# A linear-attention block with a ReLU feed-forward layer: the first four tiles loaded and normalized in another order, tile 4 transposed on TensorE, all engines' orders written anew

## The chip, the cores and the metric

The kernel runs on one core of a Trainium2 chip. The metric is device time in microseconds; a time given for a kernel is the median of its runs.

## What is computed

The input is 2048 rows of 512 bf16 values. With layer norm without weights:

```python
x = A_x
h = x + attention(layernorm(x), A_wqkv, A_wo)
h2 = h + relu(layernorm(h) @ B_w1) @ B_w2        # 512 -> 1792 -> 512

# attention, 32 heads of 16:
q, k, v = split(x @ wqkv)
phi = lambda t: where(t > 0, t + 1, exp(t)) + 1e-6
kv  = sum over rows of phi(k)^T v ;  z = sum over rows of phi(k)
o   = (phi(q) @ kv) / (phi(q) . z + 1e-6)
return o @ wo
```

## The kernel before

The 2048 rows are 16 tiles of 128 rows (128 partitions). Four tiles make a chunk of 512 rows, which is the moving operand of the matmuls that produce transposed results. Nothing is scheduled automatically: the text `ORDER` names every operation with its tile and its PSUM bank, and the program is recorded in that order. Each engine runs its own instructions strictly in that order and waits by semaphores for the others, so moving a word in the text moves it in one engine's queue (a DMA: in SyncE's) and past nothing else. A word such as `K.0.3.0.2` means operation `op_K` with tile 0, bank 3, and the contraction steps 0 and 1.

The first phase, up to about 40 us, goes through these operations for each tile t:

- `lx` (L201) loads x tiles, `lk`, `lq`, `lv`, `lo`, `l1`, `l2` (L204) load weights: wk, wq, wv, wo, w1, w2, each in halves or pieces. All DMAs are issued by SyncE (SP), in the order of the text.
- `S` (L226) and `A` (L227) on VectorE: statistics of a tile, and their aggregation to mean and variance. `R` (L232, L233) on ScalarE: the reciprocal of the standard deviation as exp(-0.5 ln(var + eps)), for one tile or for a pair in one instruction each. `N` (L251) on VectorE: the normalized tile.
- The tile transposed, as the matmuls need it: either `T` (L270), four transposes on TensorE into a PSUM bank, and `E` (L280), ScalarE's copy to SBUF; or `X` (L291), one DMA transpose issued by SyncE. Before the change tiles 0 to 3 go by T and E, tiles 4 to 15 by X.
- `K` (L299): four matmuls, k of the tile, into one of the banks 0 to 3. `F` and `U` on ScalarE (L317, L320): exp and relu of it, one bank or two at a time. `M` and `D` on VectorE (L324, L327): min(exp, 1) + 1e-6, and the sum with the relu, which is phi(k). `W` (L332) does U's and D's work in one VectorE instruction from PSUM.
- `G` (L351): four matmuls that add the tile's part of layernorm(x)^T phi(k) into the banks 4 to 7.

Ahead of the first tile `warm` (L215) does 11 matmuls on zeros. After the tiles, z and kv are formed (`z`, `kv`, `kx`), multiplied with wo (`m`), and q is computed per chunk (`Q`, L307, then `qF`, `qU`, `qM`, `qD` or `qW`, as for k). The reciprocal of the denominator is expanded to all columns by ScalarE (`dnx`, L461), transposed by DMA (`dt`, L480) or on TensorE (`rt`, copied by `re` or `rv`), and multiplied with phi(q) by VectorE (`dm`, L484); `h` (L494) multiplies that with the matrix of `m`, and `hD` (L500) adds x. The second layer norm is `s`, `a`, `r`, `n`, its transposes `x` (L292) or `t` and `e`. Then come `p` (L510, with w1), its relu `pA` on ScalarE or `pD` on VectorE (L521), `f` (L530, with w2), `fo` (L538) and the store `fd` (L545). Tile 15, the last, is done in three pieces of columns.

Of the kernel before, what the change touches and what calls it, by code (L numbers as in the profile page):

```python
# [56 lines left out]
def kernel(  # L57
# [18 lines left out]
    NT = S // P  # L76
# [11 lines left out]
    const = ctx.enter_context(tc.tile_pool(name="const", bufs=1))  # L88
    big = ctx.enter_context(tc.tile_pool(name="big", bufs=1))
# [11 lines left out]
    x_nat = big.tile([P, NT, D], BF16, name="x_nat")  # L101
# [6 lines left out]
    eps5 = const.tile([P, 1], F32, name="eps5")  # L108
# [8 lines left out]
    ln_nat = h_nat  # L117
# [10 lines left out]
    mv = big.tile([P, NT, nc.vector.BN_AGGR_DIM], F32, name="mv")  # L128
    rstd = big.tile([P, NT], F32, name="rstd")
    nmean = big.tile([P, NT], F32, name="nmean")  # L130
    st2 = big.tile([P, NT, nc.vector.BN_STATS_DIM], F32, name="st2")
    mv2 = big.tile([P, NT, nc.vector.BN_AGGR_DIM], F32, name="mv2")
    rstd2 = big.tile([P, NT], F32, name="rstd2")
# [5 lines left out]
    hn = big.tile([P, NQ, D], BF16, name="hn")  # L139
# [109 lines left out]
    def op_N(t, k=0, n=KD):  # L249
        cols = slice(k * P, (k + n) * P)  # L250
        nc.vector.tensor_scalar(  # L251
            out=ln_nat[:, t, cols], in0=x_nat[:, t, cols],
            scalar1=mv[:, t, 0:1], scalar2=rstd[:, t : t + 1],
            op0=ALU.subtract, op1=ALU.mult,
        )

    def op_n(t):
# [323 lines left out]
```

## Time and profile before

| what | us |
|---|---|
| median of 3 runs | 170.32 (169.92 to 170.33) |
| the profiled execution | 170.08 |
| its span, first to last instruction | 168.4 |
| TensorE busy | 162.7 (97%) |
| VectorE busy | 101.2 (60%) |
| ScalarE busy | 67.7 (40%) |

Times in the profile are microseconds from the start of the span. PE is TensorE, PEld its weight loads, DVE VectorE, ACT ScalarE, POOL GpSimd, SPq the queue on which SyncE issues DMAs. In the timelines a row has start, length, engine, line, operation, operands and count, and in brackets how long the engine had been idle before and what ended that. In the chain of waits a row has start, length and what held the end of the program at that time. In the list of DMA issues the last number is the time from issue to landing.

### The profile page before, as it was taken

To read this page: it belongs to the slowest core of one execution; us is meant where nothing else is said; L and a number is where in the kernel's file an instruction comes from. 1 tells how busy PE (TensorE), PEld (TensorE's weight loads), DVE (VectorE), ACT (ScalarE), POOL (GpSimd) and SP (SyncE) were. 2 spreads that over 40 slices of the span, in tenths; PEclk is the share of its full clock that TensorE was granted. 3 is DMA by queue.
4 is the path that set the end of the run, shared out by engine and by line. 5 is a ranking of instruction groups with operands and counts; after the bars stand their busy time and mean duration, and the time that the engine had idled before them with its cause. 6 is when DMAs were issued, how large, how long until landed. Compare 5 with 4: busy or idle time off the path is not lost.

```text
span 168.4 us, 2310 instructions
## 1 busy us (share of the span) xinstructions
PE 162.7 (97%) x871; PEld 76.1 (45%) x871; DVE 101.2 (60%) x202; ACT 67.7 (40%) x100; POOL 4.8 (3%) x21
## 2 busy tenths in 40 slices
PE   7699999999999999999999999999999999999993
PEld 2244443445554454544444444444444444444552
DVE  3899998997578999786967372047203600204152
ACT  3697765847879865652000504200220245000000
POOL 7300000000000000000000000000000000000000
PEclk9999999999999999999999999999999999999999
DMA  4954566899133353535130126300320000002113
GB/s 128 339 187 94 132 123 150 231 326 351 36 64 62 75 147 72 146 62 104 27 64 0 31 42 157 82 4 0 84 72 0 31 4 0 0 0 84 40 35 93
DMA packets 30491, 15.49 MB, mean 92 GB/s; under 512 B 23184, under 2 KB 29328, under 8 KB 30480
## 3 DMA queue, kind: packets, MB, share of 16 engines
q1 hardware_dynamic: 30480, 15.34, 34.5%
q8 instruction: 7, 0.11, 0.3%
q14 instruction: 4, 0.03, 0.1%
HBM read 7.86 MB, written 2.10 MB: 59 GB/s over the span
## 4 chain that ended last, share of the span: by engine, by line
PE 94%; DMA 2%; DVE 1%; SPq 0%; issue 0%
PE bk L530 29%; PE bk L510 29%; PE bk L299 9%; PE bk L351 8%; PE bk L307 8%; PE bk L494 8%; DMA x_nat<-in_A_x_dram 2%; PE bk L270 1%; PE bk L448 1%; DVE st L226 1%; PE bk L392 1%; PE bk L404 1%; SPq L201 0%; PE bk L370 0%; DVE gT L538 0%
## 5 line engine op out<-in xcount | busy, mean ns | idle before, releaser
L530 PE MATMUL bk<-w_sb,at 128*128 128x512 bf16 (+2 forms) x252 | 50.7, 355 | 0.0
L510 PE MATMUL bk<-lnT,w_sb 128*128 128x512 bf16 x224 | 50.5, 379 | 0.0
L516 ACT ACTIVATE at<-bk 128x1024 bf16<-128x1024 f32 x17 | 17.3, 1022 | 55.6 <-PE bk L510 55.6
L530 PEld LDWEIGHTS <-at 128*128 128x128 bf16 x252 | 23.5, 98 | 25.3 <-DVE at L521 0.2
L510 PEld LDWEIGHTS <-w_sb 128*128 128x128 bf16 x224 | 21.7, 98 | 26.0
L538 DVE SCALAR_TENSOR_TENSOR gT<-bk,rstd,h_nat 128x512 bf16<-128x512 f32 (+2 forms) x18 | 12.2, 690 | 31.2 <-PE bk L530 31.2
L521 DVE TENSOR_SCALAR at<-bk 128x1024 bf16<-128x1024 f32 x11 | 13.3, 1220 | 20.7 <-PE bk L510 20.4
L317 ACT ACTIVATE eb<-bk 128x1024 bf16<-128x1024 f32 (+1 forms) x18 | 16.6, 926 | 6.9 <-PE bk L299 4.2
L307 PE MATMUL bk<-lnT,wq_sb 128*128 128x512 bf16 x64 | 15.8, 379 | 0.0
L299 PE MATMUL bk<-wk_sb,lnT 128*128 128x512 bf16 x64 | 15.5, 380 | 0.0
L494 PE MATMUL bk<-m_sb,pqs 128*128 128x512 bf16 x64 | 15.3, 379 | 0.0
L351 PE MATMUL bk<-at,h_nat 128*128 128x512 bf16 x56 | 13.7, 379 | 0.0
L320 ACT ACTIVATE rb<-bk 128x1024 bf16<-128x1024 f32 (+1 forms) x14 | 12.5, 900 | 0.7 <-PE bk L307 0.7
L500 DVE TENSOR_TENSOR h_nat<-bk,x_nat 128x512 bf16<-128x512 f32 x16 | 10.6, 681 | 2.4 <-PE bk L494 2.3
L226 DVE BATCH_NORM_STATS2 st<-x_nat 128x6 f32<-128x512 bf16 x16 | 10.5, 681 | 2.4 <-DMA x_nat<-in_A_x_dram 2.4
L228 DVE BATCH_NORM_STATS2 st<-h_nat 128x6 f32<-128x512 bf16 x16 | 10.8, 684 | 0.1
L351 PEld LDWEIGHTS <-h_nat 128*128 128x128 bf16 x64 | 6.2, 97 | 7.7 <-issue 0.7
L299 PEld LDWEIGHTS <-lnT 128*128 128x128 bf16 x64 | 5.8, 98 | 8.2 <-DMA lnT<-h_nat 1.8
L494 PEld LDWEIGHTS <-pqs 128*128 128x128 bf16 x64 | 6.2, 98 | 7.0 <-DVE pqs L484 0.3
L307 PEld LDWEIGHTS <-wq_sb 128*128 128x128 bf16 x64 | 5.9, 98 | 6.4
L461 ACT ACTIVATE wk_sb<-ld 128x1024 bf16<-128x1024 f32 x8 | 8.1, 1051 | 0.1
L324 DVE TENSOR_SCALAR eb<-eb 128x1024 bf16<-128x1024 bf16 (+1 forms) x18 | 6.9, 383 | 0.9 <-ACT eb L317 0.8
(61 smaller groups left out, 89.0 us busy)
## 6 DMA issues: line engine op xcount, KB each, us to landing
out_dram<-gT SPq DMA_DIRECT2D x15, 128.0 KB, 1.9
w_sb<-in_B_w_dram SPq DMA_DIRECT2D x2, 896.0 KB, 8.4
x_nat<-in_A_x_dram SPq DMA_DIRECT2D x2, 512.0 KB, 6.6
w_sb<-in_B_w_dram SPq DMA_DIRECT2D x2, 512.0 KB, 4.6
x_nat<-in_A_x_dram SPq DMA_DIRECT2D x3, 256.0 KB, 4.2
w_sb<-in_B_w_dram SPq DMA_DIRECT2D x2, 384.0 KB, 3.4
wk_sb<-in_A_wqkv_dram SPq DMA_DIRECT2D x2, 256.0 KB, 4.0
wq_sb<-in_A_wqkv_dram SPq DMA_DIRECT2D x2, 256.0 KB, 3.0
```

What stands on the lines that cost most here:

```text
L226: op_S = lambda t: nc.vector.bn_stats(out=st[:, t, :], in_=x_nat[:, t, :])
L299: nc.tensor.matmul(bk[:, b, :], lhsT=lnT[c][:, kd, j * P : (j + 1) * P], rhs=wk_sb[:, kd, :], start=(kd == 0), stop=(kd == KD - 1),)
L307: nc.tensor.matmul(bk[:, b, :], lhsT=wq_sb[:, kd, j * P : (j + 1) * P], rhs=lnT[c][:, kd, :], start=(kd == 0), stop=(kd == KD - 1),)
L317: nc.scalar.activation(out=buf(eb, kind, i, n), in_=bank(at_bank[kind, i], n), func=ACT.Exp)
L320: nc.scalar.activation(out=buf(rb, kind, i, n), in_=bank(at_bank[kind, i], n), func=ACT.Relu)
L351: nc.tensor.matmul(bk[:, KD + kd, :], lhsT=ln_nat[:, t, kd * P : (kd + 1) * P], rhs=pk(t)[:, 0, :], start=(t == 0), stop=(t == NT - 1),)
L494: nc.tensor.matmul(bk[:, b, :], lhsT=pqs[:, (c * KD + jb) % NQ, j * P : (j + 1) * P], rhs=m_sb[:, jb, :], start=(jb == 0), stop=(jb == KD ...
L510: nc.tensor.matmul(bk[:, b, cols], lhsT=w1_sb[:, kd, f * P : (f + 1) * P], rhs=lnT[c][:, kd, cols], start=(kd == 0), stop=(kd == KD - 1),)
L516: nc.scalar.activation(out=acts[c % 2][:, f : f + n, :], in_=bank(at_bank["p", c, f], n), func=ACT.Relu)
L521: nc.vector.tensor_scalar(out=acts[c % 2][:, f : f + n, :], in0=bank(at_bank["p", c, f], n), scalar1=0.0, scalar2=None, op0=ALU.max,)
L530: nc.tensor.matmul(bk[:, b, 0 : w * P], lhsT=acts[c % 2][:, f, j * P : (j + 1) * P], rhs=w2_sb[:, f, k * P : (k + w) * P], start=(f == 0), ...
L538: nc.vector.scalar_tensor_tensor(out=o_t[:, t % NO, cols], in0=bk[:, at_bank["f", t, k], 0 : w * P], scalar=rstd2[:, t : t + 1], in1=h_nat ...
```

## The change

All tiles of the first phase go through the same operations as before, with these differences:

- Tiles 2 and 3 of x are loaded by one DMA each (`lx.2.1 lx.3.1`, before `lx.2.2`); the two halves of wk follow, now fifth and sixth in SyncE's queue.
- Tile 0 is aggregated, scaled and normalized ahead of the other tiles, and its transposes and the first half of its K stand ahead of the transposes of tile 1.
- R of tiles 2 and 3 is one pair (`R.2.2`, before `R.2.1 R.3.1`), and so are F, U, M and D of these two tiles (`F.2.2` and so on, before one bank at a time).
- Tile 4 is transposed by `T.4.3` and `E.4` instead of `X.4`.
- All queues stand in a new order to the end of the program. Among this: the first half of wq is issued right behind the x tiles and the second half ahead of X.8; wv, wo and most of w1 and w2 are issued behind the last X; `W.8.2` takes the place of U and D for tiles 8 and 9 (before, `W.14.2` for 14 and 15); one of the two copies of the Gram banks, `gA.2.2` on ScalarE, is now `gD.2.2` on VectorE; `qW` is used for other pairs; one `pA` becomes a `pD`.

The beginning of the text, before and after:

```diff
-const masks table lx.0.1 lx.1.1 lx.2.2 lk.0.2 lk.2.2 lx.4.2 lx.6.2 lx.8.4 lx.12.4 S.0 S.1 A.0 S.2 warm.1.6 A.1
-R.0.1 S.3 A.2 R.1.1 warm.9.6 N.0 A.3 N.1 R.2.1 R.3.1 N.2 N.3 warm.1.6 T.0.2 T.1.7 T.2.5 S.4 E.0 S.5 T.3.4 A.4
+const lx.0.1 lx.1.1 lx.2.1 lx.3.1 lk.0.2 lk.2.2 lx.4.2 lx.6.2 lx.8.4 lx.12.4 S.0 warm.1.1 table A.0 S.1 warm.1.1
+R.0.1 N.0 A.1 S.3 warm.9.1 S.2 T.0.5 R.1.1 A.3 A.2 E.0 N.1 K.0.0.0.2 T.1.4 R.2.2 N.2 K.0.0.2.2 N.3 S.5 E.1 F.0.1
...
```

The diff also adds a tile `ssq` and four operations (`C`, `Y`, `B`, `Nc`: statistics by ScalarE) that the new order doesn't use. They move the line numbers: T is L297, K L326, X L318, S L227, N L252, dt L507 in the changed kernel.

VectorE's queue at the start, behind four memsets, before (BN_STATS is S, BN_AGGR is A, TENSOR_SCALAR is N):

```order
L226 BN_STATS st<-x_nat 128x6 x2
L227 BN_AGGR mv<-st 128x2
L226 BN_STATS st<-x_nat 128x6
L227 BN_AGGR mv<-st 128x2
L226 BN_STATS st<-x_nat 128x6
L227 BN_AGGR mv<-st 128x2
L251 TENSOR_SCALAR h_nat<-x_nat,mv,rstd 128x512
L227 BN_AGGR mv<-st 128x2
L251 TENSOR_SCALAR h_nat<-x_nat,mv,rstd 128x512 x3
```

and in the changed kernel:

```order
L227 BN_STATS st<-x_nat 128x6
L228 BN_AGGR mv<-st 128x2
L227 BN_STATS st<-x_nat 128x6
L252 TENSOR_SCALAR h_nat<-x_nat,mv,rstd 128x512
L228 BN_AGGR mv<-st 128x2
L227 BN_STATS st<-x_nat 128x6 x2
L228 BN_AGGR mv<-st 128x2 x2
L252 TENSOR_SCALAR h_nat<-x_nat,mv,rstd 128x512 x3
```

The first normalization stands behind the statistics of two tiles, before behind those of four.

ScalarE's queue at the start, behind the table load, before (the first two lines are R, L280 is E, L317 and L320 are F and U):

```order
L232 ACTIVATE rstd<-mv,eps_73 128x1
L233 ACTIVATE rstd<-rstd 128x1
...
L280 ACTIVATE lnT_81<-bk 128x4x128 x4
L232 ACTIVATE rstd<-mv,eps_73 128x2
L233 ACTIVATE rstd<-rstd 128x2
L317 ACTIVATE eb<-bk 128x512
L320 ACTIVATE rb<-bk 128x512
```

and in the changed kernel, behind R of tiles 0 and 1:

```order
L307 ACTIVATE lnT_81<-bk 128x4x128
L233 ACTIVATE rstd<-mv,eps_73 128x2
L234 ACTIVATE rstd<-rstd 128x2
L307 ACTIVATE lnT_81<-bk 128x4x128
L344 ACTIVATE eb<-bk 128x512
L347 ACTIVATE rb<-bk 128x512
L307 ACTIVATE lnT_81<-bk 128x4x128 x2
```

Before, R of all four tiles and the four E stood ahead of the first F; now E.0 stands behind R.1, and F and U of tile 0 stand between E.1 and the pair E.2, E.3.

SyncE's queue around the transposes of the reciprocals (L480, in the changed kernel L507; w_sb with 1792 columns is w1, with 512 w2), before:

```order
L204 DMA w_sb<-in_B_w_dram 128x2x1792
L480 DMA_TRANSPOSE rd<-wk_sb 128x4x128 x6
L292 DMA_TRANSPOSE lnT_81<-hn 128x4x128 x3
L204 DMA w_sb<-in_B_w_dram 128x3x512
```

and in the changed kernel:

```order
L205 DMA wo_sb<-in_A_wo_dram 128x2x512
L507 DMA_TRANSPOSE rd<-wk_sb 128x4x128 x3
L205 DMA w_sb<-in_B_w_dram 128x2x1792
L205 DMA w_sb<-in_B_w_dram 128x4x512
L507 DMA_TRANSPOSE rd<-wk_sb 128x4x128 x3
L319 DMA_TRANSPOSE lnT_81<-hn 128x4x128 x3
```

One half of w1 and four of the fourteen pieces of w2 now stand between the third and the fourth of these transposes.

More of the change, by code (lines that the diff above doesn't have):

```diff
@@ new lines @@
+dt.0 qM.1.2.2 dt.3 mA.0.2 Q.2.3.7 Q.3.1.3 dt.1 qW.1.2.2 m.3.5 l1.0.2 dm.0.0.2 m.2.4 Q.3.0.2 l2.3.4 mA.2.2 dn.1.1
+dm.0.2.2 Q.2.2.6 h.3.5 h.0.0 h.2.4 hD.3 dnl.1 s.3 dnx.1.0.2 dnx.1.2.2 h.1.1 rt.6.5 hD.0 Q.3.2.0 qF.2.2.2
+qU.3.0.2 a.3 dt.5 s.0 qF.3.0.2 hD.1 qU.2.2.2 a.0 hD.2 dt.4 n.0 Q.3.3.1 n.3 re.6 qF.3.2.2 Q.2.0.3 dt.7 s.1
+qU.3.2.2 Q.2.1.4 dm.1.0.2 dm.1.2.2 a.1 h.4.6 qF.2.0.2 qM.2.2.2 x.0 n.1 qU.2.0.2 s.2 a.2 x.3 n.2 h.6.7 x.1 h.7.0
+hD.6 t.2.5 s.6 h.5.1 qM.2.0.2 e.2 qD.2.2.2 qD.2.0.2 p.0.10.2 p.0.5.7 hD.5 dn.2.5 p.0.2.4 hD.4 dnl.2 hD.7
@@ new lines @@
+qM.3.0.2 p.0.11.3 dnx.2.0.2 qM.3.2.2 s.4 qD.3.2.2 s.5 a.6 r.0.4 dt.8 p.0.4.6 p.0.13.1 pA.0.10.2 dnx.2.2.2
+p.0.0.2 dt.9 dt.11 p.0.1.3 p.0.12.0 pD.0.4.2 qD.3.0.2 pD.0.0.2 p.0.3.5 dt.10 dm.2.0.2 dn.3.2 dm.2.2.2 a.4
+pA.0.12.2 dnl.3 dnx.3.0.2 n.6 p.0.6.6 p.0.9.3 h.8.0 p.0.7.7 pA.0.2.2 dnx.3.2.2 h.10.4 hD.10 hD.8 dt.12 x.6 s.7
+dt.15 pA.0.6.2 p.0.8.2 dt.14 h.9.6 hD.9 s.10 h.11.0 pA.0.8.2 hD.11 f.3.2.0.7 a.7 a.5 dt.13 dm.3.0.2 f.0.4.0.7
+f.2.7.0.7 n.5 n.4 dm.3.2.2 h.12.3 h.15.1 a.10 f.3.2.7.7 hD.12 hD.15 fo.3 h.14.0 s.9 a.9 n.10 n.7 f.2.7.7.7
@@ new lines @@
+f.5.0.0.7 p.2.5.6 f.5.0.7.7 fd.6 pD.2.4.2 pD.2.2.2 p.2.12.2 fo.5 x.13 f.4.1.7.7 fo.4 p.2.13.3 fd.5 pD.2.12.2
+fd.4 fd.7 p.2.0.6 p.2.1.7 p.3.2.4 pD.2.0.2 p.3.3.5 r.8.4 p.2.10.1 p.3.0.6 p.2.11.2 pD.3.2.2 f.8.5.0.7 p.3.7.3
+f.10.4.0.7 pA.2.10.2 f.10.4.7.7 p.3.4.1 f.11.0.0.7 p.3.5.2 pA.3.4.2 f.11.0.7.7 p.3.6.2 pA.3.6.2 p.3.10.1
+f.8.5.7.7 p.3.11.2 p.3.1.7 fo.10 fo.8 p.3.12.3 pD.3.0.2 fo.11 fd.11 p.3.13.4 pA.3.12.2 pA.3.10.2 f.14.6.0.7
+f.9.0.0.7 p.3.8.2 f.9.0.7.7 p.3.9.3 pA.3.8.2 fo.9 fd.8 f.12.5.0.7 f.12.5.7.7 f.14.6.7.7 fd.10 f.13.4.0.7 fd.9
@@ L53 @@
+f.13.4.7.7 f.15.0.0.14.3.1 fo.13 fo.15.3.1 fo.14 fd.15.3.1 f.15.2.0.14.0.2 fo.12 fd.13 fd.14 fo.15.0.2
+f.15.4.0.14.2.1 fo.15.2.1 fd.12 fd.15.0.2 fd.15.2.1
 """
@@ L130 @@
     nmean = big.tile([P, NT], F32, name="nmean")
+    ssq = big.tile([P, NT], F32, name="ssq")
     st2 = big.tile([P, NT, nc.vector.BN_STATS_DIM], F32, name="st2")
@@ L254, in op_N, with op_C, op_Y, op_B @@
             op0=ALU.subtract, op1=ALU.mult,
+        )
+    def op_C(t):
+        nc.scalar.activation(
+            out=hn[:, 0, :], in_=x_nat[:, t, :], func=ACT.Copy, scale=-1.0 / D,
+            accum_out=nmean[:, t : t + 1],
+        )
+    def op_Y(t):
+        nc.scalar.activation(
+            out=hn[:, 0, :], in_=x_nat[:, t, :], func=ACT.Square, bias=nmean[:, t : t + 1], scale=1.0,
+            accum_out=ssq[:, t : t + 1],
+        )
+    def op_B(t):
+        nc.scalar.activation(
+            out=rstd[:, t : t + 1], in_=ssq[:, t : t + 1], func=ACT.Ln, bias=eps5[:], scale=1.0 / D
+        )
+        nc.scalar.activation(
+            out=rstd[:, t : t + 1], in_=rstd[:, t : t + 1], func=ACT.Exp, scale=-0.5
+        )
+    def op_Nc(t):
+        nc.vector.tensor_scalar(
+            out=ln_nat[:, t, :], in0=x_nat[:, t, :],
+            scalar1=nmean[:, t : t + 1], scalar2=rstd[:, t : t + 1], op0=ALU.add, op1=ALU.mult,
         )
```

47 lines of the change are left out of this document (15 added, 32 removed).

## The prediction

> **What bounds the kernel now.** I read the page first, then the chain of waits in order of time, then the timelines of the first 30 us.
>
> ```profile
> span 168.4 us, 2310 instructions
> ...
> PE 94%; DMA 2%; DVE 1%; SPq 0%; issue 0%
> ```
>
> TensorE holds 94% of the chain, so the time is its matmuls plus what it waits. The chain in order of time shows where it waits (start, length, what):
>
> ```profile
> 1.72 3.26 DMA x_nat<-in_A_x_dram
> ...
> 5.70 0.08 DVE mv L227
> ...
> 6.79 1.11 PE bk L270 x12
> ...
> 8.32 3.45 PE bk L299 x16
> ...
> 12.73 1.02 PE bk L351 x4
> ...
> 26.10 2.92 PE bk L299 x12
> 29.02 0.86 PE bk L351 x4
> ...
> 44.53 0.22 PE bk L270 x4
> ...
> 165.65 0.35 DVE gT L538
> ```
>
> Unhindered, four 512-wide matmuls take 0.86 (3.45 for 16) and four transposes 0.22. Pieces such as 1.02 for four, or 2.92 for twelve (2.59 at pace), were held. The same engine's timeline gives the idle time ahead of the transposes:
>
> ```profile
> 1.25 3.92 PE L215 MATMUL bk<-m_sb 128*128 128x512 bf16 x11 [1.25 <-DVE ones L177]
> 6.79 1.53 PE L270 MATMUL bk<-ident,h_nat 128*128 128x128 bf16 x16 [1.61 <-DVE h_nat L251]
> ...
> 28.86 1.03 PE L351 MATMUL bk<-at,h_nat 128*128 128x512 bf16 x4
> ```
>
> The losses are 1.61 (idle until 6.79), 0.65 (16 transposes in 1.53 instead of 0.88) and 0.85 (8.32 to 29.02 is 20.70 for 56 K and 36 G matmuls, 92 x 0.2156 = 19.85). After 29 us every piece goes at pace. So **3.1 us can be won, all of it before 29 us; later there is only something to lose.** The start waits for VectorE, which waits for tiles 2 and 3 and is then full:
>
> ```profile
> 2.99 1.29 DVE L226 BATCH_NORM_STATS2 st<-x_nat 128x6 f32<-128x512 bf16 x2 [1.77 <-DMA x_nat<-in_A_x_dram]
> ...
> 5.00 0.69 DVE L226 BATCH_NORM_STATS2 st<-x_nat 128x6 f32<-128x512 bf16 x1 [0.64 <-DMA x_nat<-in_A_x_dram]
> ...
> 6.74 1.13 DVE L251 TENSOR_SCALAR h_nat<-x_nat,mv,rstd 128x512 bf16<-128x512 bf16 x3
> ...
> 5.00:10.00 5.00, 3.36 (x26) 1.73 (x26) 4.96 (x15) 3.93 (x13) 1.00 (x4) 1.00 1.02 369
> ```
>
> The last row is a window (TensorE, weight loads, VectorE, ScalarE, GpSimd, clock, DMA share, GB/s): VectorE is busy 4.96 of 5.00. Its idle 0.64 is all that the change can give it at the start.
>
> **The loads.** Issues on SyncE's queue, and landings:
>
> ```profile
> 0.80 1.34 SPq L201 DMA_DIRECT2D x_nat<-in_A_x_dram  x3
> 2.19 0.95 SPq L204 DMA_DIRECT2D wk_sb<-in_A_wqkv_dram  x2
> ...
> x_nat<-in_A_x_dram SPq DMA_DIRECT2D x1, 128.0 KB, 2.2
> ...
> x_nat<-in_A_x_dram SPq DMA_DIRECT2D x1, 256.0 KB, 3.3
> ...
> wk_sb<-in_A_wqkv_dram SPq DMA_DIRECT2D x1, 256.0 KB, 3.9
> ```
>
> An issue takes 0.46. Tile 2, issued at 1.72, lands between 3.9 (2.2, its size) and 5.0 (3.3); tile 3, issued at 2.18, between 4.4 and 5.5. I take 2.2, the row of the same size. Everything behind is issued 0.46 later: the first weight half lands between 2.19 + 3.9 = 6.1 (bandwidth decides) and 6.55 (issue decides); I take 6.3 and carry 0.2 both ways.
>
> On splitting, the Trainium skill speaks against it ("DMA: Bandwidth & Descriptors", Rules for kernel authors): coalesce small transfers, since each pays a fixed cost. By that rule alone every later load is one issue late, the late end of the range; the two sizes above, 2.2 and 3.3, show the other side, that the half lands 1.1 sooner.
>
> **The walk to 29 us.** Durations on ScalarE:
>
> ```profile
> 4.39 0.29 ACT L232 ACTIVATE rstd<-mv,eps 128x1 f32<-128x1 f32 x1 [2.31 <-DVE mv L227]
> 4.72 0.20 ACT L233 ACTIVATE rstd<-rstd 128x1 f32<-128x1 f32 x1
> ...
> 7.33 2.04 ACT L280 ACTIVATE lnT<-bk 128x512 bf16<-128x512 bf16 x4
> ...
> 9.76 0.58 ACT L317 ACTIVATE eb<-bk 128x512 bf16<-128x512 f32 x1
> 10.23 0.59 ACT L320 ACTIVATE rb<-bk 128x512 bf16<-128x512 f32 x1
> ```
>
> R (two instructions) takes 0.53; E, F and U follow each other every 0.48. On VectorE, S follows S every 0.60 (two in 1.29, one in 0.69), N every 0.33 (three in 1.13), and an A adds 0.08.
>
> 1. A.0 now follows S.0 (ends 3.68): A.0 3.69, R.0 3.89 to 4.42, N.0 4.46 to 4.84. T.0 needs TensorE, whose warm-up runs until 5.0: 5.0 to 5.2 instead of 6.79. E.0 ends at 6.0, K.0's first half starts with the weights at 6.3.
> 2. VectorE goes on without its 0.64: A.1, S.3 4.85, S.2 5.45, both A by 6.30. R for the pair 6.34 to 6.87, so N.2 waits 0.33 behind N.1; N.2 6.91, N.3 ends 7.63. T.3 stands ahead of T.2 and starts at 7.68; K.1 runs 8.13 to 9.0.
> 3. ScalarE: E.1 7.25, F.0, U.0, E.2 8.69, E.3 9.17 to 9.78. So K.2's half 9.35, K.3 9.83 to 10.70.
> 4. VectorE: S.5 at 7.7 (its tile landed at 7.4 and may be 0.46 later), S.4, M.0, S.6, three A, D.0 10.0 to 10.42. G.0 10.70 to 11.56; the chain had it at 11.78, but after two K matmuls more.
> 5. S.7, N.5 10.95 to 11.36, N.4 ends 11.75. T.4 11.8 to 12.0, K.2's rest to 12.45, E.4 ends 12.83, K.4 12.87 to 13.73.
> 6. A DMA transpose lands 2.5 after its N:
>
> ```profile
> 10.33 8.24 SPq L291 DMA_TRANSPOSE lnT<-h_nat  x6
> ...
> lnT<-h_nat SPq DMA_TRANSPOSE x1, 2.5
> ```
>
> X.5 lands at 13.9 and, one every 1.3, X.6 at 15.2 and X.7 at 16.5. K.5, G.1, K.6, K.7 end at 14.8, 15.65, 16.5 and 17.4. D.2, behind S.12, S.13, N.8, N.9 on VectorE, ends at 17.3, just in time for G.3. From there 13 groups of four (G.3, G.2, K.8 to G.8, K.11, K.10) find their input there: 17.4 + 13 x 0.863 = 28.62.
>
> Before, the same 14 K and 9 G were done at 28.86. **The sum is -0.24**, T.4's own 0.22 (row at 44.53) included; 0.2 either way from the weights and from S.5. What is won at 5 us (1.8) is nearly all given back: 1.1 to the wait for the weights, the rest to VectorE and ScalarE, which were full before.
>
> The Trainium skill ("TensorE: Matmul & The Clock Gate", Part 4) gives a 128x128 transpose as about 275 ns within a kernel; four for tile 4 would be 1.1 and the sum +0.6, slower. The row at 44.53 says 0.22 for four, so I give that a chance of about nothing.
>
> From 29 us on I count nothing: the same matmuls in another order, at pace before. Two operations move to VectorE, which takes 1.22 to read two PSUM banks:
>
> ```profile
> L521 DVE TENSOR_SCALAR at<-bk 128x1024 bf16<-128x1024 f32 x11 | 13.3, 1220 | 20.7 <-PE bk L510 20.4
> ```
>
> The copy of two Gram banks would run from 41.2 to 42.4 while TensorE does Q.1.1 (0.86); without that cover kv waits 0.3. The relu-and-add for tiles 8 and 9 delays N.14 and N.15 by at most its 1.2; in the walk, with it, their transposes land by 29.7 and are used at 31; if that second is gone, K.14 pays the rest. The tail has the same three last pieces of tile 15 and one more store queued ahead of the last; SyncE catches up by the last result, else one issue, 0.45.
>
> The profiled execution took 170.08 (span 168.4 and 1.7 around it), 0.24 under the median 170.32 of the runs shown. The forecast is 169.84 against its own, **170.1** against the median (169.85 to 170.3).
>
> **Rivals.** What this kernel's measurement can tell from no change is about 0.3%, 0.5 us.
>
> *Faster.* The two idle pieces that I put on VectorE (0.33 ahead of N.2, up to 0.3 ahead of S.5) need not appear if R and the loads come early; handed on through D.2 they make it -0.5 to -0.85, 169.5 to 169.8. For it: the 0.64 is real. Against: N.2 waits for R of the pair by dependence. Chance 0.22.
>
> *Slower: transposes behind weights.* The change issues 896 KB of w1 and 512 KB of w2 on SyncE between the third and fourth transpose of the reciprocals; before, nothing stood there:
>
> ```profile
> 49.89 2.00 ACT L461 ACTIVATE wk_sb<-ld 128x1024 bf16<-128x1024 f32 x2
> ...
> 50.98 3.81 SPq L480 DMA_TRANSPOSE rd<-wk_sb  x3
> ...
> 56.13 1.29 DVE L484 TENSOR_TENSOR pqs<-pqT,rd 128x1024 bf16<-128x1024 bf16 x2
> ...
> 57.30 1.67 PE L494 MATMUL bk<-m_sb,pqs 128*128 128x512 bf16 x7
> ```
>
> 1408 KB at 369 GB/s are 3.8 us, from 49 to 52.8; the fourth transpose is due at 51. The product at 56.13 waits for the last of the three, and the h matmuls at 57.3 for half of the product (0.65): there are only 0.5 us to spare, 0.3 after my gain. For it, one earlier case, three transposes that took 5.37 to issue and 4.7 to land behind 256 KB of wv:
>
> ```profile
> 20.68 0.57 SPq L204 DMA_DIRECT2D wv_sb<-in_A_wqkv_dram  x1
> 21.34 5.37 SPq L291 DMA_TRANSPOSE lnT<-h_nat  x3
> ...
> lnT<-h_nat SPq DMA_TRANSPOSE x1, 4.7
> ```
>
> Against: two behind 384 KB of w2 at 65.65 were issued in 2.50, at pace:
>
> ```profile
> 65.65 0.58 SPq L204 DMA_DIRECT2D w_sb<-in_B_w_dram  x1
> 66.33 2.50 SPq L480 DMA_TRANSPOSE rd<-wk_sb  x2
> ```
>
> If the fourth has to wait for the weights, h.4 waits 0.6 to 1.5, say 0.9: net +0.65, 170.97. It decides from 0.3 us of delay on. Chance 0.20.
>
> *Slower: X.8 behind wq.* The second half of wq is now ahead of X.8. With the 4.7 of that row instead of 2.5, X.8 lands at 20.6 where K.8 is due at 19.1: 1.5 lost, +1.26, 171.6. Chance 0.08.
>
> *The change does not do what it says.* Tile 3 lands at 5.5 instead of 4.4: S.3 starts later than it did, VectorE's 0.64 stays, the sum is +0.1 to +0.4, about 170.5. Chance 0.07.
>
> *Other waits after 29 us,* each new order having some with a half us to spare (for p.2: X.9 follows a relu of p.1): over +0.5, chance 0.05.
>
> **How the numbers follow.** Forecast 0.38, faster 0.22, transposes behind weights 0.20, X.8 0.08, no effect 0.07, others 0.05. Faster by over 0.3%: 0.22. Within: 0.38 + 0.07 = 0.45. Slower: 0.20 + 0.08 + 0.05 = 0.33. The range goes from 169.5, the faster rival's end, to 171.2, past the first slower one; it leaves out X.8, some of the others and the edges, under 0.2.
>
> **What would show it.** First transpose at 5.0 with four in 0.22; first K matmul at 6.1 to 6.55, the difference deciding bandwidth or issue; no idle on VectorE between 4.3 and 6.2; N.2 after a gap of 0.3; the G that follows K.10 at 28.6; after that no held piece in the chain. Wrong would be: S.3 later than 5.0, a K piece near 19 longer than 0.86, an idle TensorE at 57 with the transposes of the reciprocals issued over more than 3.8 us.

## The result, and the profile after

| kernel | median, us | runs |
|---|---|---|
| before | 170.82 (169.92 to 172.02) | 20 |
| after | 171.80 (170.47 to 173.01) | 20 |

The change made the kernel slower: ratio after to before 1.0046, 95% interval 1.0023 to 1.0068. The profiled execution of after took 171.80 us, its own median. That of before (170.08) was 0.74 under the median of the 20 runs.

The span and the chain's shares, from the page of after:

```profile
span 170.1 us, 2286 instructions
...
PE 86%; DMA 5%; DVE 5%; SPq 2%; issue 1%
```

TensorE's share of the chain fell from 94 to 86%: until 20 us the end is now held by a load, VectorE and a DMA transpose. The chain of waits in order of time (start, length, what):

```profile
3.65 5.05 DMA x_nat<-in_A_x_dram
...
8.73 1.29 DVE st L227 x2
...
16.94 3.35 DMA lnT<-h_nat
...
20.34 1.90 PE bk L326 x8
...
166.71 0.35 DVE gT L565
```

The first row is the load of tiles 4 and 5, issued at 3.65 and landed at 8.7; the third is X.8, 3.35 from issue to landing behind the second half of wq. TensorE's timeline (in brackets the idle time before a row, and what ended it):

```profile
1.25 4.34 PE L216 MATMUL bk<-m_sb 128*128 128x512 bf16 x11 [1.25 <-DVE ones L178]
5.43 0.39 PE L297 MATMUL bk<-ident,h_nat 128*128 128x128 bf16 x4
6.71 0.59 PE L326 MATMUL bk<-wk_sb,lnT 128*128 128x512 bf16 x2 [0.89 <-DMA wk_sb<-in_A_wqkv_dram]
...
11.39 1.02 PE L378 MATMUL bk<-pk_lo,h_nat 128*128 128x512 bf16 x4 [0.18 <-DVE pk_lo L354]
12.70 0.40 PE L297 MATMUL bk<-ident,h_nat 128*128 128x128 bf16 x4 [0.29 <-ACT rstd L233]
...
13.79 2.13 PE L326 MATMUL bk<-wk_sb,lnT 128*128 128x512 bf16 x8 [0.26 <-ACT lnT L307]
...
28.12 1.89 PE L326 MATMUL bk<-wk_sb,lnT 128*128 128x512 bf16 x8
29.84 1.46 PE L334 MATMUL bk<-lnT,wq_sb 128*128 128x512 bf16 x6
```

T.0 starts 1.36 us sooner than before (5.43 instead of 6.79), but what follows is full of small waits, and K.10 is done at 29.84; the matching point stood at 28.86 before and at 28.62 in the forecast. VectorE's timeline shows where it slips:

```profile
3.23 0.69 DVE L227 BATCH_NORM_STATS2 st<-x_nat 128x6 f32<-128x512 bf16 x1 [2.00 <-DMA x_nat<-in_A_x_dram]
...
7.22 0.73 DVE L252 TENSOR_SCALAR h_nat<-x_nat,mv,rstd 128x512 bf16<-128x512 bf16 x2 [0.30 <-ACT rstd L234]
8.73 1.29 DVE L227 BATCH_NORM_STATS2 st<-x_nat 128x6 f32<-128x512 bf16 x2 [0.77 <-DMA x_nat<-in_A_x_dram]
```

The 0.30 ahead of N.2 is the forecast one; S.5 starts at 8.73, not at 7.7, after 0.77 of waiting for its tile.

The second place is the end. In the last rows of VectorE of before, the results `fo` come one by one as their matmuls end:

```profile
160.38 0.75 DVE L538 SCALAR_TENSOR_TENSOR gT<-bk,rstd,h_nat 128x512 bf16<-128x512 f32 x1 [3.11 <-PE bk L530]
161.83 0.75 DVE L538 SCALAR_TENSOR_TENSOR gT<-bk,rstd,h_nat 128x512 bf16<-128x512 f32 x1 [0.70 <-PE bk L530]
163.34 1.01 DVE L538 SCALAR_TENSOR_TENSOR gT<-bk,rstd,h_nat 128x512 bf16<-128x512 f32 x2 [0.76 <-PE bk L530]
164.87 0.48 DVE L538 SCALAR_TENSOR_TENSOR gT<-bk,rstd,h_nat 128x256 bf16<-128x256 f32 x1 [0.52 <-PE bk L530]
165.65 0.35 DVE L538 SCALAR_TENSOR_TENSOR gT<-bk,rstd,h_nat 128x128 bf16<-128x128 f32 x1 [0.30 <-PE bk L530]
```

and on SyncE's queue the last store is issued at 166.03, when the last result is done (165.65 + 0.35):

```profile
166.03 0.37 SPq L545 DMA_DIRECT2D out_dram<-gT  x1
```

The last rows of VectorE of after:

```profile
163.68 2.81 DVE L565 SCALAR_TENSOR_TENSOR gT<-bk,rstd,h_nat 128x512 bf16<-128x512 f32 x5 [7.72 <-PE bk L557]
166.71 0.35 DVE L565 SCALAR_TENSOR_TENSOR gT<-bk,rstd,h_nat 128x128 bf16<-128x128 f32 x1 [0.23 <-PE bk L557]
```

and SyncE's of after, the last six stores in one row and the last of them in a row of its own:

```profile
164.78 3.35 SPq L572 DMA_DIRECT2D out_dram<-gT  x6
...
167.72 0.41 SPq L572 DMA_DIRECT2D out_dram<-gT  x1
```

VectorE stands idle for 7.72 us and then does five results in a row. In the text, `fo.13` stands ahead of `fo.14` and `fo.12`, although tile 13's matmuls end last of the three, so two finished tiles wait behind it. Their stores leave together, six in 3.35 us, and the last is issued at 167.72, 0.66 after its result (166.71 + 0.35). Before, that was 0.03. In the other five traces of kernels with this end the last store follows its result by 0.29 to 0.87 (0.45 in a second trace of after), in all eight traces with before's end by 0.03. The Trainium skill ("PSUM — Partial Sum Buffer", Engine vs sequencer instructions) says that VectorE's queue is strictly first in, first out; the 7.72 us agree.

### The profile page after: what moved, and what is told of

Read it like the earlier page. It is cut to its first block, busy times and chain, and to the rows that moved or that the text cites. A ratio compares the mean times of both kernels' runs of the same rounds, so it can differ in the third digit from the quotient of the medians.

```text
span 170.1 us, 2286 instructions
## 1 busy us (share of the span) xinstructions
PE 162.5 (96%) x859; PEld 76.2 (45%) x875; DVE 102.4 (60%) x202; ACT 65.7 (39%) x95; POOL 4.9 (3%) x21
## 4 chain that ended last, share of the span: by engine, by line
PE 86%; DMA 5%; DVE 5%; SPq 2%; issue 1%
PE bk L537 28%; PE bk L557 28%; PE bk L334 8%; PE bk L521 8%; PE bk L378 6%; PE bk L326 4%; DMA x_nat<-in_A_x_dram 3%; DVE st L227 3%; DMA lnT<-h_nat 2%; DVE h_nat L252 1%; SPq L202 1%; PE bk L475 1%; SPq L205 1%; PE bk L419 1%; PE bk L431 1%
## 5 line engine op out<-in xcount | busy, mean ns | idle before, releaser
L543 ACT ACTIVATE at<-bk 128x1024 bf16<-128x1024 f32 x16 | 16.1, 1021 | 70.2 <-PE bk L537 70.2
L548 DVE TENSOR_SCALAR at<-bk 128x1024 bf16<-128x1024 f32 x12 | 14.5, 1218 | 13.5 <-PE bk L537 13.4
L326 PE MATMUL bk<-wk_sb,lnT 128*128 128x512 bf16 x63 | 16.0, 380 | 1.5 <-DMA wk_sb<-in_A_wqkv_dram 0.9
L334 PE MATMUL bk<-lnT,wq_sb 128*128 128x512 bf16 x61 | 15.0, 379 | 0.2
L378 PE MATMUL bk<-at,h_nat 128*128 128x512 bf16 x55 | 13.2, 379 | 0.1
L227 DVE BATCH_NORM_STATS2 st<-x_nat 128x6 f32<-128x512 bf16 x16 | 10.5, 680 | 2.8 <-DMA x_nat<-in_A_x_dram 2.8
L326 PEld LDWEIGHTS <-lnT 128*128 128x128 bf16 x64 | 5.6, 97 | 9.4 <-ACT lnT L307 2.7
L511 DVE TENSOR_TENSOR pqs<-pqT,rd 128x1024 bf16<-128x1024 bf16 x8 | 5.2, 686 | 4.0 <-DMA rd<-wk_sb 4.0
```

What stands on the lines that cost most here:

```text
L227: op_S = lambda t: nc.vector.bn_stats(out=st[:, t, :], in_=x_nat[:, t, :])
L326: nc.tensor.matmul(bk[:, b, :], lhsT=lnT[c][:, kd, j * P : (j + 1) * P], rhs=wk_sb[:, kd, :], start=(kd == 0), stop=(kd == KD - 1),)
L334: nc.tensor.matmul(bk[:, b, :], lhsT=wq_sb[:, kd, j * P : (j + 1) * P], rhs=lnT[c][:, kd, :], start=(kd == 0), stop=(kd == KD - 1),)
L378: nc.tensor.matmul(bk[:, KD + kd, :], lhsT=ln_nat[:, t, kd * P : (kd + 1) * P], rhs=pk(t)[:, 0, :], start=(t == 0), stop=(t == NT - 1),)
L543: nc.scalar.activation(out=acts[c % 2][:, f : f + n, :], in_=bank(at_bank["p", c, f], n), func=ACT.Relu)
L548: nc.vector.tensor_scalar(out=acts[c % 2][:, f : f + n, :], in0=bank(at_bank["p", c, f], n), scalar1=0.0, scalar2=None, op0=ALU.max,)
```

## The experiments

Each ratio is to before, run on the same chip; the medians of before were 170.82 to 171.37 in the different sets. Each set ran on another chip, and after itself was run for the result and in the second set only, so in the other sets an edit of after is compared with it across chips.

**First set: the loads.** My theory was that splitting the load delays the ones behind it and wq delays X.8. Tiles 2 and 3 by one load again, in after:

```diff
-lx.2.1 lx.3.1
+lx.2.2
```

> The changed kernel with tiles 2 and 3 loaded by one DMA again. Theory, loads: the additional issue puts tiles 4 and 5 back, for which VectorE waited 0.77 us at 8.7 us (they landed at 8.70, before the change at 7.4); so they land 0.5 to 1.2 earlier, that wait goes, and the time falls by 0.4 to 0.8, to about the kernel before. Rival, order: the loss lies in the queues behind the first four tiles (tile 4 on TensorE, the second half of wq ahead of X.8); then the time stays within 0.3 of the changed kernel. S.3 waits for both tiles here, at most 0.1 later.

171.49, ratio 1.0019 (0.9997 to 1.0041), against 1.0046. S.5 on VectorE's timeline of this kernel, with no wait ahead of it (tiles 4 and 5 landed at 7.66):

```profile
8.29 1.28 DVE L227 BATCH_NORM_STATS2 st<-x_nat 128x6 f32<-128x512 bf16 x2
```

and K.8 on TensorE's, still held by X.8 for 0.43:

```profile
20.24 1.90 PE L326 MATMUL bk<-wk_sb,lnT 128*128 128x512 bf16 x8 [0.43 <-DMA lnT<-h_nat]
```

Then wq's second half behind X.13, in after:

```diff
-lq.2.2 S.10 G.3 G.2 X.8
+S.10 G.3 G.2 X.8
...
-X.13 R.14.2
+X.13 lq.2.2 R.14.2
```

> The changed kernel with the second half of wq issued behind X.13 instead of ahead of X.8. In the trace of the changed kernel X.8 landed at 20.29, 3.35 us after its issue, and TensorE waited 0.26 for it. Theory, X.8 behind wq: X.8 lands 0.6 to 1.0 earlier, the wait goes and the time falls by 0.2 to 0.3. Rival, loads: VectorE's queue is what holds the chain there; the time stays within 0.1.

171.30, ratio 1.0001 (0.9974 to 1.0027); X.8 landed 2.7 after its issue instead of 3.35, with no wait of TensorE for it. And the split alone, put into before:

```diff
-lx.2.2
+lx.2.1 lx.3.1
```

> The kernel before with tiles 2 and 3 loaded by two DMAs, nothing else. Theory, loads: everything behind lands 0.5 to 1.2 later; the kernel before has slack for its weights (first used at 8.2) and for tiles 4 and 5 (first used at 7.8, landed at 7.4), so VectorE waits 0.1 to 0.8 at S.4, and the time rises by 0.1 to 0.6, while S.2 starts up to 0.9 earlier. Rival, order: S.2 earlier decides, the time falls by 0.2 to 0.6.

170.58, ratio 0.9961 (0.9941 to 0.9982): **faster**, against my theory, though the trace shows what it said, the late landing on VectorE's timeline:

```profile
8.69 1.29 DVE L226 BATCH_NORM_STATS2 st<-x_nat 128x6 f32<-128x512 bf16 x2 [0.96 <-DMA x_nat<-in_A_x_dram]
```

and the wait that follows on TensorE's:

```profile
12.58 1.02 PE L351 MATMUL bk<-pk_lo,h_nat 128*128 128x512 bf16 x4 [0.94 <-DVE pk_lo L327]
```

Something else had to be won. The last kernel of the set, after with tiles 4 and 5 ahead of the weights:

```diff
-lk.0.2 lk.2.2 lx.4.2
+lx.4.2 lk.0.2 lk.2.2
```

> The changed kernel with the load of tiles 4 and 5 issued ahead of the two halves of wk. Theory, loads: S.5 starts at about 7.7 instead of 8.7, the first K matmul 0.6 to 0.7 later than 6.7; as D.0 and N.5 hang on VectorE, the time falls by 0.2 to 0.6. Rival, weights: the first K matmul is what decides; the time rises by 0.3 to 0.6. Rival, order: within 0.2.

172.24, ratio 1.0067 (1.0036 to 1.0098). Tiles 4 and 5 landed at 6.47, but TensorE now waits twice for weights, and then its matmuls slow down, in the profiled run:

```profile
7.73 0.59 PE L326 MATMUL bk<-wk_sb,lnT 128*128 128x512 bf16 x2 [1.58 <-DMA wk_sb<-in_A_wqkv_dram]
8.16 0.39 PE L297 MATMUL bk<-ident,h_nat 128*128 128x128 bf16 x4
8.95 0.98 PE L326 MATMUL bk<-wk_sb,lnT 128*128 128x512 bf16 x2 [0.40 <-DMA wk_sb<-in_A_wqkv_dram]
9.72 1.06 PE L297 MATMUL bk<-ident,h_nat 128*128 128x128 bf16 x8
```

Two K matmuls take 0.98 instead of 0.59, eight transposes 1.06 instead of 0.62: the granted clock halved after the idle stretch (its mean from 7 to 13 us was 0.72 in this run; in 2 of the 11 runs the mean over the whole execution was 0.99 or less). The runs of before, taken one by one, show the same: their mean granted clock is either 0.988 to 0.99 or nearly 1.0. In this set 22 of 34 had the lower one, with a median of 171.46 against 170.83; over all sets 67 of 144, dearer by 0.6 to 1.1 us. After never had it (0.996 or more in 32 runs), nor had before with two loads.

**Second set: the clock.** Before once more, for a second trace:

> The kernel before, unchanged, for a trace that is nearer to its median than the one shown (170.08 us, where 34 later runs had a median of 171.37). Clock theory: of those 34 runs 22 had a mean granted clock of 0.988 to 0.99, with a median of 171.46 us, and 12 had 0.999 to 1.0, with a median of 170.83; so TensorE runs for some us at half speed in most runs of before, after the idle time between the warm-ups and T.0 (1.61 us in the trace shown). It expects, in a profiled run of 171 us or more, matmuls at 427 ns and transposes at 107 ns somewhere between 7 and 13 us, where the trace shown had 216 and 55, and the last PE matmul to start 0.6 to 1.0 us later than the 165.40 of the trace shown. Landing theory: the one load of tiles 2 and 3 lands near 5.5 us (as in the run with one load) and not at 4.98 as in the trace shown, T.0 starts 0.5 later, at 7.3, and everything else is 0.5 later with matmuls at 216 ns.

171.44 in the profiled run, clock 0.99, as in 8 of the 10 runs. TensorE's timeline of this run:

```profile
7.43 1.85 PE L270 MATMUL bk<-ident,h_nat 128*128 128x128 bf16 x16 [2.08 <-DVE h_nat L251]
9.08 4.71 PE L299 MATMUL bk<-wk_sb,lnT 128*128 128x512 bf16 x16
```

and the windows from 7 to 13 us of the two runs of before, the first shown and this one (TensorE's busy time, weight loads, VectorE, ScalarE, GpSimd; then the granted clock):

```profile
7.00:13.00 6.00, 5.94 (x38) 2.74 (x36) 5.86 (x19) 5.90 (x17) 0.00 (x0) 1.00 0.64 216
```

```profile
7.00:13.00 6.00, 5.57 (x30) 3.08 (x31) 5.18 (x17) 4.62 (x13) 0.00 (x0) 0.72 0.64 228
```

Both theories hold here. Tiles 2 and 3 landed at 5.62 instead of 4.98, so T.0 starts at 7.43 instead of 6.79. The idle time ahead of it is 2.08 instead of 1.61, and the clock falls to half for 3.4 us (half speed for 3.4 of the 6 us gives the mean of 0.72): 16 K matmuls take 4.71 instead of 3.62. The Trainium skill ("TensorE: Matmul & The Clock Gate", Why this matters for your kernels) warns of idle gaps above some 3 us; here 2.08 was enough, and 1.61 was not in the trace shown.

If that idle time costs the clock, five more warm-ups in before must win it back:

```diff
-warm.1.6 T.0.2
+warm.6.6 T.0.2
```

> Before, with five more warm-up matmuls behind the eleven, so that TensorE's idle time ahead of T.0 shrinks by 5 x 0.216 = 1.1 us, and nothing else changed. Clock theory: the loss of granted clock in most runs of before follows from that idle time; without it all runs have 0.995 or more, and the ratio is 0.996 to 0.998 (the median of before's own runs with full clock over that of all: 170.83 to 171.37), as with the two loads. Landing theory (the two loads made before faster because tile 2 was there sooner): no change, 1.000, and the clock 0.99 in more than half of the runs as before.

170.22, ratio 0.9954 (0.9931 to 0.9977), clock 0.999 or more in all 12 runs. The row of the warm-ups and that of the transposes:

```profile
1.25 5.85 PE L215 MATMUL bk<-m_sb 128*128 128x512 bf16 x16 [1.25 <-DVE ones L177]
6.94 1.49 PE L270 MATMUL bk<-ident,h_nat 128*128 128x128 bf16 x16
```

With the clock kept, before is about as fast as with two loads (0.9961). The clock explains a part of both gains, not all: against only those runs of before that kept the full clock on the same chip, the warm-ups are still 0.51 faster (170.22 to 170.73) and the two loads 0.25 (170.58 to 170.83). On this chip this version beats both kernels. Run once more in the fifth set it gave 0.9976 (0.9947 to 1.0006), 170.26, where only 7 of 23 runs of before had the low clock. There the other 16 have a median of 170.25, the same, so whether the warm-ups win anything besides the clock stays open:

> The kernel with five more warm-up matmuls, unchanged, to set beside the one with after's end on the same chip. If its gain belongs to the program: ratio 0.993 to 0.998 to before, full clock in all runs, 170.0 to 170.5 us. If it was the first chip's: 1.000.

In the second set also after unchanged, and after with both edits of the loads (one load, wq behind X.13):

> The kernel after, unchanged, on the chip of the three others, so that it can be set beside them. If its loss of 0.46% belongs to the program: a ratio of 1.002 to 1.007 to before, granted clock 0.996 or more in all runs. If it was a matter of the first chip, a ratio within 0.998 to 1.002. Both expect the landing of tiles 4 and 5 at 8.5 to 9.2 us and X.8 landed after 20 us.

171.60, ratio 1.0040 (1.0017 to 1.0062), clock 0.996 or more throughout.

> After, with tiles 2 and 3 by one load again and with wq's second half issued behind X.13 instead of ahead of X.8: the two edits that alone gave 1.0019 and 1.0001 where after has 1.0046. Theory of the loads (each edit removes a delay of its own: the split's on tiles 4 and 5, wq's on X.8): they add, 1.0046 - 0.0027 - 0.0045 = 0.997, tiles 4 and 5 landed at 7.4 to 7.7 us, X.8 landed before 20 us without PE waiting for it, last PE matmul at 165.8 to 166.0. Rival (the front's stalls are set by the end of the warm-ups and the transposes through ScalarE, and the two edits' figures differ from after's by the chip alone): the same as the better of the two, 1.000 to 1.002, last PE matmul at 166.3 or later.

171.44, ratio 1.0028 (1.0008 to 1.0047). The two edits didn't add up to 0.997: against after on the same chip 1.2 us were expected and 0.16 came. The means differ by 0.28 (95% interval -0.07 to 0.63). So the loads alone were not the main cause. Its trace still had a span end 3.5 us behind the start of the last matmul, as all kernels with after's end had (3.2 to 3.9), where those with before's end had 3.0 to 3.1.

**Third set: the tail, and the parts by themselves.** After with the last results in the order in which their matmuls end:

```diff
-fd.9 f.13.4.7.7 f.15.0.0.14.3.1 fo.13 fo.15.3.1 fo.14 fd.15.3.1 f.15.2.0.14.0.2 fo.12 fd.13 fd.14 fo.15.0.2
-f.15.4.0.14.2.1 fo.15.2.1 fd.12 fd.15.0.2 fd.15.2.1
+fd.9 fo.12 fd.12 fo.14 fd.14 f.13.4.7.7 f.15.0.0.14.3.1 fo.13 fd.13 fo.15.3.1 fd.15.3.1 f.15.2.0.14.0.2 fo.15.0.2
+f.15.4.0.14.2.1 fo.15.2.1 fd.15.0.2 fd.15.2.1
```

> After, with the last results and stores in another order and nothing else: fo.12 and fo.14 (whose matmuls end some 3 and 1.5 us before tile 13's) ahead of fo.13 on VectorE, and each store right behind its result. Tail theory: in six traces of kernels with after's end the span ends 3.2 to 3.9 us behind the start of the last matmul (3.65 in after's own), in four with before's end 2.9 to 3.1, because five results wait on VectorE behind fo.13 until 163.7 and six stores of about 0.5 us each then queue on SyncE behind one another, so that the last one is issued 1.27 us behind the start of the last matmul instead of 0.64. The edit wins 0.5 to 0.65 us: ratio 1.000 to 1.0015 where after had 1.0040 and 1.0046, and the last store is issued 0.65 us behind the start of the last matmul. Rival (the loss of after lies in the front alone and something else closes the span): ratio 1.003 to 1.006.

171.01, ratio 1.0007 (0.9974 to 1.0040). The last result on VectorE:

```profile
167.25 0.35 DVE L565 SCALAR_TENSOR_TENSOR gT<-bk,rstd,h_nat 128x128 bf16<-128x128 f32 x1 [0.23 <-PE bk L557]
```

and the last store on SyncE:

```profile
167.62 0.33 SPq L572 DMA_DIRECT2D out_dram<-gT  x1
```

The store follows its result by 0.02 again. Against all runs of before the loss is gone; against the 14 of them with the full clock (median 170.62) 0.39 is left. The interval is wide and overlaps that of after, so the tail was tried the other way round in the fifth set: before with more warm-ups, whose times lie close together, and **after's end**.

```diff
-fo.14 fo.12 fo.13 fo.15.3.1 fd.12 f.15.1.0.14.2.1 fd.13
-fd.15.3.1 fd.14 fo.15.0.2 fd.15.0.2 fo.15.2.1 fd.15.2.1
+fo.13 fo.15.3.1 fo.14 fd.15.3.1 f.15.1.0.14.2.1 fo.12
+fd.13 fd.14 fo.15.0.2 fo.15.2.1 fd.12 fd.15.0.2 fd.15.2.1
```

> Before with five more warm-up matmuls and with after's end: on VectorE fo.13 ahead of fo.14 and fo.12, their stores behind, tile 12's store between the last two results' and theirs; nothing else. A kernel whose times lie close together (170.0 to 170.8 without the edit) and whose front is not after's. Tail theory: the last store waits on SyncE behind five others, 0.5 to 0.65 us slower than the same kernel without the edit, 170.7 to 170.9 where that has 170.2; the span ends 3.4 to 3.7 us behind the start of the last matmul instead of 2.97. Rival (the 0.6 of a_tail came by chance of the runs, or by something in after's front): no difference, within 0.15 us.

171.18 (170.43 to 171.78), where the same kernel without the edit had 170.26 (169.81 to 170.63) on the same chip. The means of the two sets of 12 are 171.12 and 170.26, a difference of 0.87 (95% interval 0.59 to 1.15), more than the 0.5 to 0.65 expected. Its ratio to before is 1.0023 (0.9995 to 1.0051). VectorE's last row:

```profile
163.85 2.98 DVE L538 SCALAR_TENSOR_TENSOR gT<-bk,rstd,h_nat 128x512 bf16<-128x512 f32 x6 [6.13 <-PE bk L530]
```

and SyncE's last stores:

```profile
164.89 2.78 SPq L545 DMA_DIRECT2D out_dram<-gT  x6
...
167.26 0.41 SPq L545 DMA_DIRECT2D out_dram<-gT  x1
```

Here VectorE does all six in a row, so the last result (done at 163.85 + 2.98 = 166.83) waits on VectorE as well as its store on SyncE (0.43). An end in which `fo.13` holds the other results thus costs time with nothing of after's front. Its 0.87 is more than the same order costs in after: here the last result starts 0.64 behind the last matmul (165.84), 0.38 more than in after (0.26), and only the wait on SyncE is after's too.

All three edits (tail, one load, wq) in after:

> After with three edits: the order of the tail, tiles 2 and 3 by one load, wq's second half behind X.13. The two others gave 1.0028 together where after on the same chip gave 1.0040. If all of it adds: 1.0028 - 0.0033 = 0.9995 (0.998 to 1.001), with the last PE matmul at 165.6 to 166.3 and the span's end 3.0 us behind it. Rival (one load and wq are worth nothing beside the tail): the same as the kernel with the tail alone within 0.1%.

170.47, ratio 0.9978 (0.9953 to 1.0002): with the tail mended, the two edits of the loads bring another 0.54 against the kernel with the tail alone. On this one chip the means of the two sets of 12 runs differ by 0.64 (95% interval 0.24 to 1.04), so they do bring something; between this and the 0.16 above their worth stays open. Beside the kernel with the two edits of the loads alone, 1.0028 (1.0008 to 1.0047) on the other chip, this is a second test of the tail in after's own order: the two intervals don't overlap.

The split alone, without the clock in play (before with more warm-ups, tiles 2 and 3 by two loads):

> Before with five more warm-up matmuls (ratio 0.9954, granted clock full in all runs) and with tiles 2 and 3 by two loads: the price of the split alone, with the clock out of play. Loads theory: tiles 4 and 5 land at 8.5 to 9.2 us instead of 7.9, VectorE's statistics of them and with them the first product start later, TensorE waits up to 0.9 us ahead of G.0 as it did in the trace of before with two loads: 0.4 to 0.7 us slower than with the warm-ups alone, ratio 0.998 to 0.9995. Rival (two loads are a gain by themselves, as the 0.9961 of before with two loads would have it, since tile 2 is there 1 us sooner): 0.9955 or below. In between (0.996 to 0.997): it is worth nothing either way, and the 0.9961 was the clock alone.

170.32, ratio 0.9967 (0.9937 to 0.9997) beside 0.9954: worth nothing that the runs can tell. In its trace tiles 4 and 5 landed at 7.85. Over all traces with this order of loads, they landed at 7.41 to 7.93 in 10 of 11 with one load (8.71 in the eleventh), and at 8.66 to 9.29 in 5 of 6 with two. So the split makes a late landing likely and not certain.

The price of tile 4 on TensorE, in the same kernel:

```diff
-G.0 D.3.1 G.3 F.2.1 F.1.1
+G.0 D.3.1 G.3 T.4.1 F.2.1 E.4 F.1.1
...
-X.5 X.4 M.2.1
+X.5 M.2.1
...
-K.5.1 R.8.2 K.4.0
+K.4.0 R.8.2 K.5.1
```

> Before with five more warm-up matmuls, and tile 4 transposed by TensorE behind G.3 (one copy by ScalarE) instead of by a DMA; K.4 ahead of K.5. Price theory: T.4's 0.22 us on TensorE and E.4's 0.48 on ScalarE are on the path, as in after, where TensorE waits 0.29 for tile 4's deviation and 0.26 for E.4: 0.2 to 0.7 us slower than with the warm-ups alone, ratio 0.9966 to 0.9995. Rival (the DMA transposes are what holds TensorE before 29 us, by pieces of 0.07 to 0.16; without X.4 each lands 1.3 us sooner, and that pays for T.4): 0.9955 or below, no piece held for a DMA.

172.51, ratio 1.0098 (1.0062 to 1.0134). This is not T.4's price. K.4, now ahead of K.5, waits for ScalarE's U.1, which still reads its PSUM bank:

```profile
16.62 1.89 PE L299 MATMUL bk<-wk_sb,lnT 128*128 128x512 bf16 x8 [2.15 <-ACT rb L320]
```

The row shows one thing more. These 2.15 us of idle TensorE are longer than the 2.08 that cost before its clock, and the clock stays: eight matmuls take 1.89, as they do at full clock, and the mean was 1.0 in all 6 runs. So the length of an idle stretch alone doesn't decide. Here it came after 7 us of work (7.29 to 14.47), in before right behind the warm-ups; which difference counts, no run shows.

The edit was mended in a fourth set, with T.4 between G.0 and G.3, E.4 behind F.2, and K.5 and K.4 where they were:

> The price of tile 4 on TensorE once more. The kernel ahead of it had moved K.4 ahead of K.5, and K.4's PSUM bank was still being read for tile 1 (2.15 us of TensorE's time behind ScalarE's U.1), so its 1.0098 was no price of T.4. Here, in before with five more warm-up matmuls, T.4 stands between G.0 and G.3, its copy behind F.2 on ScalarE, and K.5 and K.4 stay where they were; X.4 is gone. Price theory: T.4's own 0.22 us and what its copy (0.48) delays on ScalarE: 0.2 to 0.5 us slower than with the warm-ups alone, ratio 0.9966 to 0.9985. Rival (it is paid for by the transposes behind X.5, each 1.25 us sooner, and by ScalarE's idle 0.74): 0.9945 to 0.996.

170.73, ratio 0.9994 (0.9967 to 1.0021) beside 0.9954 and 0.9976: 0.5 us dearer by the medians, 0.7 or 0.3 by the ratios, with intervals that overlap, on three chips. TensorE's timeline shows T.4's own 0.22 (13.22 to 13.45) and 0.43 of waiting for the same bank, which U.1 frees later since E.4 stands ahead of it on ScalarE:

```profile
13.22 0.39 PE L270 MATMUL bk<-ident,h_nat 128*128 128x128 bf16 x4
...
15.76 1.02 PE L299 MATMUL bk<-wk_sb,lnT 128*128 128x512 bf16 x4 [0.43 <-ACT rb L320]
```

Last, 8 warm-ups instead of 11 in the kernel with the three edits, since T.0 starts when they end:

```diff
-warm.9.1
+warm.6.1
```

> The kernel with after's order and the three edits (tail, one load, wq later: 0.9978), with 8 warm-up matmuls instead of 11. In after and its relatives T.0 starts where the warm-ups end, at 5.1 to 6.1 us, by how many of the 11 ran at 427 ns (7 to 11), and K.0 at 6.7 to 7.1 although the first weights land at 6.3 to 6.7. Warm-up theory: T.0 starts with N.0's end, at 5.2 to 5.4, in every run, K.0 with the weights, 0.3 to 0.5 us sooner: ratio 0.995 to 0.9965. Clock rival (TensorE needs the whole row of warm-ups to be granted the full clock): the clock is granted late, K and transposes run at 427 and 107 ns until 8 to 9 us, mean clock under 0.995 in most runs: ratio 1.000 to 1.006.

170.90, ratio 0.9994 (0.9963 to 1.0025), the clock at 0.99 in 4 of 12 runs. In the profiled run the clock held, but T.0 didn't come sooner:

```profile
1.25 3.59 PE L216 MATMUL bk<-m_sb 128*128 128x512 bf16 x8 [1.25 <-DVE ones L178]
5.50 0.40 PE L297 MATMUL bk<-ident,h_nat 128*128 128x128 bf16 x4 [0.66 <-DVE h_nat L252]
```

The first tile had landed at 3.50 in this run, and T.0 waits 0.66 for N.0. The clock rival was right for a third of the runs; the warm-up theory's gain isn't there.

## Why the prediction was wrong

I forecast 170.1, no change, and gave slower a chance of 0.33. The result is slower by 0.46%, outside the range.

**The step that failed is the tail, a term put at nothing; the second is a term of the walk, the landing of tiles 4 and 5.** The prediction put the tail as "SyncE catches up by the last result, else one issue, 0.45", and counted nothing. The traces show 0.63 more between the last result and its store (0.66 against 0.03) in the profiled run of after, and 0.42 in its second; taking it away in after brought the ratio from 1.0040 and 1.0046 to 1.0007, and putting such an end into the other kernel cost 0.87, a part of that on VectorE. The prediction went by the stores in SyncE's queue and not by VectorE's, where a result that is late holds back two that are ready. I had written that after 29 us there is only something to lose, and yet gave the loss no term.

**The base was a rare execution.** I set the sum against 170.08, "0.24 under the median 170.32 of the runs shown". It was 0.74 under the median of 20 runs: full clock, which about half of the runs lack, and tiles 2 and 3 landed at 4.98, where six later traces with one load and before's order had 5.08 to 5.75. Against the 21 runs of before with full clock in the second set (170.73) after lost 0.87 (171.60), against all (171.11) 0.49. What after gained was of a kind that the prediction doesn't have: TensorE starts early enough to keep its clock.

**The walk** ended 1.22 late (29.84 for 28.62). By its steps: T.0 at 5.43 for 5.0, since 9 warm-ups and not 7 ran at half clock, and tile 0 landed at 3.2 for 3.0; K.0 with the weights at 6.71 for 6.3; N.2 after its 0.30 as said; S.5 at 8.73 for 7.7, its term mis-sized, as I let the load be late by 0.46 and it was 1.3; from that G.0 at 11.39 for 10.70, and K.4 at 13.79 for 12.87. The runs with tiles 4 and 5 at 7.66 to 7.88 show that this was not all: X.5 landed at 14.3 to 14.8 in them too, 13.9 in the forecast. X.8 behind wq, a rival at 0.08, came about in small: 3.35 for 2.5, 0.26 of TensorE's time. Taking the full-clock runs as the measure, the whole front cost 0.87 - 0.63 = 0.24, or 0.45 with the second trace's 0.42; the 0.39 that the kernel with the mended tail has left agrees. The forecast was a gain of 0.24. Against all runs of before the front gained 0.49 - 0.63 = -0.14. That this is near the forecast is luck, by errors that cancel: a walk that came late, and a clock that wasn't counted. With the tail and the loads both mended the kernel stands at 170.47, 0.15 under the 170.62 of before's full-clock runs on its chip. So the tail and the loads (the split and wq) make up most of the miss. The trace of that kernel has tiles 4 and 5 at 8.71 all the same, so how much of it is their landing isn't shown.

**Right** was that an early T.0 is given back to the wait for the weights and to a full VectorE, and that the weights ahead of the fourth transpose of the reciprocals would most likely cost nothing. Three transposes were issued at pace behind them, on SyncE's timeline of after:

```profile
51.95 3.81 SPq L507 DMA_TRANSPOSE rd<-wk_sb  x3
```

and TensorE's h matmuls start with no idle time ahead:

```profile
58.28 2.75 PE L521 MATMUL bk<-m_sb,pqs 128*128 128x512 bf16 x11
```

What stays open: why the load behind the split lands late in most traces and not in all, how the front's loss divides between the loads, T.4 and ScalarE, and what besides the clock made before faster with more warm-ups in the second set.

## What to carry to other kernels

Read the end of the order on every engine, not on the last queue alone: on an engine that works in order, a result whose input comes late holds back those that are ready, and their stores then queue in front of the last one. Before a sum is set against a trace, ask how common that execution is: the granted clock of each run, where it is listed, tells of losses that the one trace doesn't show. And an early idle stretch of TensorE can cost time behind it as well as within it: the runs of before whose clock fell were dearer by 0.6 to 1.1 us. Filling it with matmuls on zeros won 0.46% here (0.24% in the fifth set, with an interval that reaches no change), where the reordering lost 0.46%.

## What the runs showed of the hardware

- The granted clock fell to half for about 3.4 us after 2.08 us of idle TensorE right behind the warm-ups (second run of before) and after 1.58 and 0.40 with little between them (tiles 4 and 5 first). In before it fell in 67 of 144 runs, in the kernels with more warm-ups (0.72 us of idle at most ahead of the first transposes in their traces) in none of 66. One of these had 2.15 us of idle time at 14.5 us and kept its clock. With 8 warm-ups and waits of 0.66 and 0.74 in the one trace it fell in 4 of 12 runs.
- How many warm-up matmuls ran at half clock (427 ns from start to start instead of 216) changed from run to run: 7 of 11 in the traces of before, 10 or all of 11 in that of after with one load, 14 of 16 in that with tile 4 on TensorE and K.5 and K.4 where they were.
- A load behind a split one landed 0.7 to 1.9 us later in 5 of 6 traces, though it was issued only 0.47 later (3.65 instead of 3.18).
